# A WKV state stage with two gated layers on one core: the start and five steps ordered by hand, the weights' remainder and low bits on other engines

## The chip, the cores and the metric

The kernel runs on one core of one Trainium2 chip. The metric is the device time of one execution in microseconds (us). A profile of one execution is read beside it.

## What is computed

Three stages follow each other: a recurrence over 768 time steps for 4 batches and 8 heads of size 48, a layer with a hard gate, and a layer with a norm and a silu gate. Everything is in fp32.

```python
for t in range(S):                                   # S = 768, D = 48
    cur = einsum('bhd,bhe->bhde', u * k[t], v[t])
    y[t] = einsum('bhd,bhde->bhe', r[t], state + cur)
    state = w[t][..., None] * state + einsum('bhd,bhe->bhde', k[t], v[t])
x = y as (3072, 384)
h = x @ w_in                                         # 384 x 2048
x = (h * clip(h + 3, 0, 6) / 6) @ w_out              # 2048 x 384
xn = x / sqrt(mean(x * x) + 1e-6) * rms_g
g = xn @ w_gate                                      # 384 x 1536
out = (silu(g) * (xn @ w_val)) @ w_out2              # 1536 x 384
```

## The kernel before, in words

The 768 time steps are cut into six token blocks c of 128 steps; with four batches b that is 24 state blocks (class `Job`, block c, batch b), and 512 tokens for each c. A state block runs: `scans` (two running products of w on VectorE), `muls` (r and k scaled by them, VectorE), `fill` (ScalarE writes the diagonal into the matrix a, eight heads), `pe_a` (products of r and k on TensorE, in the PSUM tile aps), `choose` (VectorE copies the valid triangle of aps into a), `pe_y` (TensorE), `copy_y` and `split`. The state itself is added to by `pe_kt`, `copy_kt`, `pe_u` and `add_u`, and scaled by `decay` on GpSimd. For c = 0 there is no earlier state: `pe_y0` and `split_y0` take the place of `pe_y`, `copy_y` and `split`, and the bonus comes from `pairs` and `pe_bonus`.

Each fp32 matmul operand is used as a pair, a rounded high part and the remainder. A product is then three matmuls (`PASS`: high x high, high x remainder, remainder x high), nine for three slices of 128. Activations are split by `emit_split` (high copy on ScalarE, subtraction on GpSimd). The weights are stored as 64-bit floats: the input arrays are bits, and class `Weight` rebuilds the fp32 value of a 128x768 slice from two 32-bit words. `load` (SP queue) fetches `raw` (two buffers). `scale` is a ScalarE product of the high word into `mag` (one buffer). `bits` has three VectorE operations: the low word shifted right by 29 (line 143), the sign bit (line 144), and the shifted `mag` joined to it (line 146), in `x` (two buffers). `parts` writes the high copy (ScalarE, line 151) and the remainder (GpSimd, line 152) into `wpair` or `bpair`. There are 16 slices for the first layer (`wa`), 18 for the second (`wb`).

The first layer goes in steps n, one for each block c and slice f (128 of the 2048 columns): `ff1` (nine matmuls into hps, line 342; relu on ScalarE, line 348; product on VectorE, line 349; split) and, two steps later, `ff2` (nine matmuls into the three accumulators o, line 361). `LAGS` = (5, 8, 0, 0, 0, 0): in the first token block slices 0 to 4 are run first for tokens 0 to 255 (steps 0 to 4), then for tokens 256 to 511 (steps 5 to 9), as half steps; steps 10 to 20 take all 512 tokens. Step 21 is the first of the second token block.

The order on each engine is written out by hand. `pin` chains all instructions of an engine in the order in which the program emits them, and each engine works through its queue in that order. Ahead of the loop three `run` lines order state blocks 0 and 1 and weights 0 and 1. In the loop the lists `before[n]`, `between[n]` and `behind[n]` say what is emitted ahead of step n's matmuls, behind its split, and behind the older step's `ff2`. `plan(j, n)` puts a state block of c > 0 into them: scans at n, products at n + 1, fill at n + 2, choose behind step n + 2, y at n + 3, split at n + 5. The blocks of c = 1 are planned at 11, 15, 19 and 23. `begun` gives the step in which a weight is rebuilt.

The six PSUM pools: ps_h two banks (hps, and yps of `pe_y0`), ps_o three (accumulators), ps_s one (small products), ps_a two (aps, yps).

In the sixth token block, and in the first gated one (lines 621 to 655), the slices of the second layer are rebuilt in the same way, among the steps.

Of the kernel before, what the change touches and what calls it, by code (L numbers as in the profile page):

```python
# [9 lines left out]
F32 = mybir.dt.float32  # L10
# [26 lines left out]
def kernel(  # L37
# [86 lines left out]
    class Weight:  # L124
# [11 lines left out]
        def scale(self):  # L136
            self.mag = st_p.tile([128, 2 * DM], F32, tag="mag", name="mag", bufs=1)
            nc.scalar.activation(out=self.mag, in_=self.words()[1].bitcast(F32), func=AF.Copy, scale=2.0 ** -112)  # L138

        def bits(self):  # L140
            low, high = self.words()
            x = st_p.tile([128, 2 * DM], U32, tag="x", name="x")
            nc.vector.tensor_scalar(x, low, 29, None, ALU.logical_shift_right)  # L143
            nc.vector.scalar_tensor_tensor(  # L144
                out=x, in0=high, scalar=0x80000000, in1=x, op0=ALU.bitwise_and, op1=ALU.bitwise_or)
            nc.vector.scalar_tensor_tensor(  # L146
                out=x, in0=self.mag.bitcast(U32), scalar=3, in1=x, op0=ALU.logical_shift_left, op1=ALU.bitwise_or)
            self.x = x.bitcast(F32).rearrange("p (a n) -> p a n", a=2)
# [9 lines left out]
    class Job:  # L158
# [19 lines left out]
        def scans(self):  # L178
            nc.vector.memset(dd[:, :, :, 0:1], 1.0)
            self.scan(0)  # L180
            self.s1, self.s2 = self.w[:, 0], self.w[:, 1]
            nc.vector.reciprocal(out=dd[:, :, :, 0:1], in_=self.s1[:, :, :, HF:HF + 1])
            self.scan(1)

# [61 lines left out]
        def pe_a(self):  # L246

            self.aps = ps_a.tile([128, 2, NP, CH], F32, tag="A", name="aps")
            for p in range(NP):
                for i in range(2):  # L250
                    nc.tensor.matmul(  # L251
                        self.aps[:, i, p, :], self.rk[64 * i:64 * i + D, p, 1:3, :].rearrange("p a j -> p (a j)"),
                        self.rk[64 * i:64 * i + D, p, 0:4:3, :], start=True, stop=True)

        def choose(self):
            for i in range(2):
                nc.vector.copy_predicated(
                    self.a[:, i], mask.unsqueeze(1).to_broadcast([128, NP, CH]), self.aps[:, i])
# [73 lines left out]
        def split_y0(self):  # L332
            xt = self.xt()
            nc.scalar.activation(out=xt[:, :, 0, :], in_=self.yps, func=AF.Copy)
# [10 lines left out]

    def emit_act(ps, n):
        a = rg_p.tile([128, n], F32, tag="a", name="a", bufs=2)
# [392 lines left out]
```

## Time and profile before

| | |
|---|---|
| time, median of 3 runs | 1035.52 us (1034.21 to 1036.18) |
| profiled execution | 1035.39 us, span 1033.6 us |
| TensorE busy | 972.1 us (94% of the span) |
| VectorE busy | 482.4 us |
| GpSimd busy | 441.8 us |
| ScalarE busy | 405.5 us |
| mean granted clock of TensorE | 0.969 |

The span runs from the first to the last instruction. In the profile PE is TensorE's matmuls, PEld its weight loads, DVE VectorE, ACT ScalarE, POOL GpSimd, SPq the DMA queue of SyncE. A busy share is an average over stages with different limits, so the stages are read one by one. A clock of 1.00 stands for 2.4 GHz, 0.50 for 1.2 GHz.

### The profile page before, as it was taken

Reading aid. Unit: us, or ns where it says so; the run is one execution under the profiler, and the core shown is the slowest. Engines: PE = TensorE matmul, PEld = TensorE weight load, DVE = VectorE, ACT = ScalarE, POOL = GpSimd, SP = SyncE. Lnnn points to the kernel's source line nnn. Section 1 sums busy time; section 2 is a strip of 40 time slices with the busy share of each in tenths; the row PEclk is TensorE's granted clock in tenths of the full one; section 3 lists DMA queues with packets and bytes.
Section 4 is the critical chain, followed back from the end, with each engine's and each line's share of the span. In section 5 each row is a group of like instructions: output and inputs, shape, how many; then the busy total and the mean of one; then the engine's idle time right before and its main releaser. Section 6 shows DMA issues by size and latency. Waiting matters only on the chain.

```text
span 1033.6 us, 14038 instructions
## 1 busy us (share of the span) xinstructions
PE 972.1 (94%) x5517; PEld 804.5 (78%) x5517; DVE 482.4 (47%) x597; ACT 405.5 (39%) x774; POOL 441.8 (43%) x361
## 2 busy tenths in 40 slices
PE   5588799899999999999998899999999999999998
PEld 4587588778888888877776677888888888888887
DVE  7858865564457556655378666412112112112111
ACT  3365365544544544454454535322222212222222
POOL 1346675455465665664375555411122112211121
PEclk9589889899999999999999989999999999999999
DMA  8236422434222422330333332010100100100000
GB/s 313 90 123 224 151 90 83 141 112 140 77 77 84 168 75 77 124 129 8 130 131 101 135 97 88 37 56 1 59 2 1 62 1 1 62 1 1 31 1 30
DMA packets 32417, 85.65 MB, mean 83 GB/s; under 512 B 5728, under 2 KB 12768, under 8 KB 32352
## 3 DMA queue, kind: packets, MB, share of 16 engines
q1 hardware_dynamic: 32352, 84.76, 23.7%
q8 instruction: 43, 0.70, 0.3%
q14 instruction: 22, 0.18, 0.0%
HBM read 71.37 MB, written 9.44 MB: 78 GB/s over the span
## 4 chain that ended last, share of the span: by engine, by line
PE 73%; DVE 10%; issue 6%; ACT 5%; POOL 2%; DMA 2%; SPq 1%; ACTq 0%; POOLq 0%; DVEq 0%
PE o L361 26%; PE hps L342 13%; PE gps L342 13%; PE vps L342 13%; DVE x L144 3%; PE aps L251 2%; PE yps L293 2%; DVE x L146 2%; DVE x L143 2%; ACT a L348 1%; POOL wpair L152 1%; DVE a L349 1%; PE yps L287 1%; ACT a L232 1%; DVE w L174 1%
## 5 line engine op out<-in xcount | busy, mean ns | idle before, releaser
L361 PE MATMUL o<-g,wpair 128*128 128x512 f32 (+1 forms) x1422 | 330.5, 377 | 1.8 <-DVE x L376 1.7
L361 PEld LDWEIGHTS o<-g,wpair 128*128 128x128 f32 x1422 | 252.6, 191 | 50.2 <-DVE x L376 2.1
L342 PE MATMUL hps<-xt,wpair 128*128 128x512 f32 (+1 forms) x981 | 221.5, 371 | 15.8 <-DVE a L349 8.7
L355 POOL TENSOR_TENSOR g<-a,g 128x512 fp32r<-128x512 f32 (+1 forms) x109 | 141.1, 1295 | 204.8 <-ACT g L354 194.4
L355 POOL TENSOR_TENSOR g<-s,g 128x512 fp32r<-128x512 f32 x72 | 95.8, 1330 | 299.1 <-ACT g L354 298.7
L342 PEld LDWEIGHTS hps<-xt,wpair 128*128 128x128 f32 x981 | 173.1, 193 | 49.5 <-DVE a L349 11.3
L636 DVE TENSOR_TENSOR s<-s,vps 128x512 f32<-128x512 f32 x72 | 49.5, 687 | 309.2 <-PE vps L342 289.8
L349 DVE SCALAR_TENSOR_TENSOR a<-a,hps 128x512 f32<-128x512 f32 (+1 forms) x109 | 67.5, 619 | 170.1 <-ACT a L348 170.0
L348 ACT ACTIVATE a<-hps,half 128x512 f32<-128x512 f32 (+1 forms) x109 | 68.6, 629 | 98.6 <-PE hps L342 93.9
L342 PE MATMUL gps<-xt,wpair 128*128 128x512 f32 x432 | 105.9, 389 | 0.0
L342 PE MATMUL vps<-xt,wpair 128*128 128x512 f32 x432 | 105.7, 389 | 0.0
L354 ACT ACTIVATE g<-a 128x512 fp32r<-128x512 f32 (+1 forms) x109 | 63.4, 581 | 107.6 <-DVE a L349 106.1
L354 ACT ACTIVATE g<-s 128x512 fp32r<-128x512 f32 x72 | 45.5, 632 | 146.1 <-DVE s L636 146.1
L633 ACT ACTIVATE s<-gps 128x512 f32<-128x512 f32 x72 | 42.9, 596 | 150.3 <-PE gps L342 150.3
L342 PEld LDWEIGHTS gps<-xt,wpair 128*128 128x128 f32 x432 | 81.0, 188 | 17.2 <-ACT s L633 0.5
L342 PEld LDWEIGHTS vps<-xt,wpair 128*128 128x128 f32 x432 | 81.1, 188 | 16.8
L152 POOL TENSOR_TENSOR wpair<-x,wpair 128x768 fp32r<-128x768 f32 x28 | 56.6, 2021 | 67.7 <-ACT wpair L151 67.7
L174 DVE TENSOR_TENSOR_SCAN w<-w,dd 128x520 f32<-128x520 f32 x48 | 80.0, 1666 | 4.5 <-DMA w<-in_dram 2.8
L361 PE MATMUL o<-g,bpair 128*128 128x512 f32 x216 | 55.2, 400 | 5.9 <-ACT x L378 3.8
L232 ACT ACTIVATE a<-iperm,cb 128x128 f32<-128x128 f32 x192 | 58.5, 387 | 0.1
L342 PE MATMUL gps<-xt,bpair 128*128 128x512 f32 x216 | 54.6, 398 | 0.2 <-ACT s L633 0.2
L138 ACT ACTIVATE mag<-raw 128x768 f32<-128x768 f32 x34 | 30.5, 897 | 59.1 <-issue 29.5
(75 smaller groups left out, 967.5 us busy)
## 6 DMA issues: line engine op xcount, KB each, us to landing
raw<-in_dram SPq DMA_DIRECT2D x34, 768.0 KB, 4.3
w<-in_dram SPq DMA_DIRECT2D x24, 520.0 KB, 3.8
rk<-in_dram SPq DMA_DIRECT2D x24, 512.0 KB, 4.5
rks<-in_dram SPq DMA_DIRECT2D x20, 384.0 KB, 4.7
v<-in_dram SPq DMA_DIRECT2D x24, 256.0 KB, 4.8
xn<-x SPq DMA_DIRECT2D x6, 768.0 KB, 4.3
xraw<-xn SPq DMA_DIRECT2D x6, 768.0 KB, 5.1
out_dram<-osb SPq DMA_DIRECT2D x15, 256.0 KB, 2.5
```

The source lines that it names most:

```text
L144: nc.vector.scalar_tensor_tensor(out=x, in0=high, scalar=0x80000000, in1=x, op0=ALU.bitwise_and, op1=ALU.bitwise_or)
L152: nc.gpsimd.tensor_tensor(out=self.dst[:, :, 1, :], in0=self.x, in1=self.dst[:, :, 0, :].bitcast(F32), op=ALU.subtract)
L174: nc.vector.tensor_tensor_scan(out=x, data0=x, data1=dd.rearrange("p a h j -> p (a h j)"), initial=0.0, op0=ALU.mult, op1=ALU.add)
L232: nc.scalar.activation(out=self.head(h), in_=iperm, func=AF.Copy, scale=self.cb[:, h, :])
L342: nc.tensor.matmul(ps, slot[:, l, k * 128:(k + 1) * 128], xt[:, k, r, :], start=(k == 0 and j == 0), stop=(k == KT - 1 and j == 2))
L348: nc.scalar.activation(out=a, in_=ps, func=AF.Relu, scale=1.0 / 6.0, bias=half)
L349: nc.vector.scalar_tensor_tensor(out=a, in0=a, scalar=1.0, in1=ps, op0=ALU.min, op1=ALU.mult)
L354: nc.scalar.activation(out=g[:, 0, :], in_=a, func=AF.Copy)
L355: nc.gpsimd.tensor_tensor(out=g[:, 1, :], in0=a, in1=g[:, 0, :].bitcast(F32), op=ALU.subtract)
L361: nc.tensor.matmul(acc[m][:, cols], slot[:, l, m * 128:(m + 1) * 128], g[:, r, :], start=(first and j == 0), stop=(last and j == 2), **kw)
L633: nc.scalar.activation(out=s, in_=gp, func=AF.Silu)
L636: nc.vector.tensor_tensor(out=s, in0=s, in1=vp, op=ALU.mult)
```

## The change

Six things are changed.

- The remainder of a weight (`rest`) is subtracted on VectorE; before it was on GpSimd (in `parts`).
- The low word's bits come from ScalarE: `scale` adds a Copy of byte 3 of each 64-bit element, times 1/32, minus 31/64, rounded to an integer into `x`. VectorE's `bits` has two operations, `sign` and `join`.
- The order ahead of the loop is written out anew, for all four state blocks of c = 0, five weights and the steps 0 to 4; the loop begins at step 5. A step is a class, `Step`, whose parts can be placed one by one.
- State block 1 has aps in two banks of the accumulators.
- `decay`, `pe_kt`, `copy_kt` of state blocks 0 to 3 stand at steps 5 to 8 (before: from step 1), `pe_u` and `add_u` one step later.
- The later weights are rebuilt at other steps (`begun`), with high copy and remainder two steps after the bits and ahead of the next weight's scaling; the state blocks of c = 1 are planned at 10, 14, 18 and 22.

```diff
         def scale(self):
             self.mag = st_p.tile([128, 2 * DM], F32, tag="mag", name="mag", bufs=1)
             nc.scalar.activation(out=self.mag, in_=self.words()[1].bitcast(F32), func=AF.Copy, scale=2.0 ** -112)
+            self.x = st_p.tile([128, 2 * DM], U32, tag="x", name="x")
+            top = self.raw.bitcast(mybir.dt.uint8).rearrange("p (n h) -> p n h", h=8)[:, :, 3]
+            nc.scalar.activation(out=self.x, in_=top, func=AF.Copy, scale=1.0 / 32, bias=-31.0 / 64)
+
+        def sign(self):
+            nc.vector.scalar_tensor_tensor(
+                out=self.x, in0=self.words()[1], scalar=0x80000000, in1=self.x,
+                op0=ALU.bitwise_and, op1=ALU.bitwise_or)
+
+        def join(self):
+            nc.vector.scalar_tensor_tensor(
+                out=self.x, in0=self.mag.bitcast(U32), scalar=3, in1=self.x,
+                op0=ALU.logical_shift_left, op1=ALU.bitwise_or)
+            self.x = self.x.bitcast(F32).rearrange("p (a n) -> p a n", a=2)
 
         def bits(self):
-            low, high = self.words()
-            x = st_p.tile([128, 2 * DM], U32, tag="x", name="x")
-            nc.vector.tensor_scalar(x, low, 29, None, ALU.logical_shift_right)
...
-        def parts(self):
+            self.sign()
+            self.join()
+
+        def high(self):
             nc.scalar.activation(out=self.dst[:, :, 0, :], in_=self.x, func=AF.Copy)
-            nc.gpsimd.tensor_tensor(
+
+        def rest(self):
+            nc.vector.tensor_tensor(
                 out=self.dst[:, :, 1, :], in0=self.x, in1=self.dst[:, :, 0, :].bitcast(F32), op=ALU.subtract)
...
         def pe_a(self):
-            self.aps = ps_a.tile([128, 2, NP, CH], F32, tag="A", name="aps")
+            if self.i == 1:
+                self.aps = [ps_o.tile([128, NP, CH], F32, tag=f"o{i}", name="aps") for i in range(2)]
+            else:
+                ps = ps_a.tile([128, 2, NP, CH], F32, tag="A", name="aps")
+                self.aps = [ps[:, i] for i in range(2)]
...
-    before[0] += [j2.pairs, j2.muls]
-    between[0] += [j2.pe_bonus, j2.fill, j2.pe_a]
-    before[1] += [j3.scans, j2.choose]
-    between[1] += [j2.pe_y0, j2.split_y0]
-    before[2] += [j3.pairs, j3.muls]
-    between[2] += [j3.pe_bonus, j3.fill, j3.pe_a]
-    behind[2] += [j3.choose]
-    between[3] += [j3.pe_y0, j3.split_y0]
-    for j, n in enumerate((1, 2, 3, 4)):
-        behind[n] += [jobs[j].decay]
-        between[n + 1] += [jobs[j].pe_kt, jobs[j].copy_kt]
-        between[n + 2] += [jobs[j].pe_u, jobs[j].add_u]
-    for j, n in zip(range(B, 2 * B), (11, 15, 19, 23)):
+    for j, n in enumerate((5, 6, 7, 8)):
+        behind[n] += [jobs[j].decay, jobs[j].pe_kt, jobs[j].copy_kt]
+        between[n + 1] += [jobs[j].pe_u, jobs[j].add_u]
+    for j, n in zip(range(B, 2 * B), (10, 14, 18, 22)):
         plan(j, n)
...
-    begun = {f: f - 2 for f in range(2, W1 + 1)} | {8: 7} | {f: f + 1 for f in range(9, F1)}
+    begun = {5: 5, 6: 7, 7: 9} | {f: f + 2 for f in range(8, F1)}
     for f, n in begun.items():
+        before[n + 2] += [wa[f].high, wa[f].rest]
         before[n] += [wa[f].scale]
         behind[n] += [wa[f].bits]
-        before[n + 1 if f < 5 else n + 2] += [wa[f].parts]
         if f + 2 < F1:
             behind[n] += [wa[f + 2].load]
-    behind[7] += [lambda: jobs[4].load("w", "rk", "rks", "v")]
-    behind[9] += [lambda: jobs[5].load("w", "rk", "v")]
+    behind[5] += [lambda: jobs[4].load("w", "rk", "rks", "v")]
+    behind[8] += [lambda: jobs[5].load("w", "rk", "v")]
...
-    run((j0.scans, j0.pairs, j0.pe_bonus, j0.muls, j0.fill, j0.pe_a, j1.scans, j1.pairs, j1.pe_bonus, j1.muls))
-    run((j0.choose, j1.fill, j1.pe_a, j0.pe_y0, wa[0].scale, wa[0].bits, j1.choose, j1.pe_y0))
-    run((j0.split_y0, wa[0].parts, wa[1].scale, wa[1].bits, j1.split_y0, j2.scans, wa[1].parts))
+    w0, w1, w2, w3, w4 = wa[:5]
+    line = [Step(*x) for x in steps]
+    s0, s1, s2, s3, s4 = line[:5]
+    run((j0.scans, j0.pairs, j0.pe_bonus, j0.muls, j0.fill, j0.pe_a))
+    run((j1.scans, j1.pairs, w0.scale, j1.pe_bonus, j1.fill, j1.muls, j1.pe_a))
+    run((w0.sign, j0.choose, w0.join, w2.load, w0.high, j0.pe_y0, j1.choose, j1.pe_y0))
+    run((w0.rest, j0.high_y0, j0.rest_y0, w1.scale, w1.sign, j1.high_y0, j1.rest_y0, s0.pe_h, s0.relu))
+    run((w1.join, w3.load, w1.high, j2.scan1, w1.rest, s1.pe_h, s0.act, s0.split, s1.relu, j2.scan2, j2.pairs))
+    run((j2.pe_bonus, w2.scale, j2.muls, j2.fill, j2.pe_a, w2.sign, w2.join, w4.load, s1.act, s1.split, w2.high))
+    run((j2.choose, j2.pe_y0, w2.rest, s2.pe_h, s2.relu, s0.pe_o, j3.scans, j2.high_y0, j2.rest_y0, j3.pairs))
+    run((j3.pe_bonus, w3.scale, j3.muls, j3.fill, j3.pe_a, s2.act, s2.split, w3.bits, wa[5].load, w3.high))
+    run((j3.choose, j3.pe_y0, w3.rest, s3.pe_h, s3.relu, s1.pe_o, w4.scale, w4.bits, wa[6].load, w4.high))
+    run((j3.high_y0, s3.act, s3.split, j3.rest_y0, w4.rest, s4.pe_h, s4.relu, s2.pe_o, s4.act, s4.split))
+    todo += [s3, s4]
     pin()
 
-    for n, (c, f, cols) in enumerate(steps):
-        if n == W1:
+    for n in range(LAGS[0], len(steps)):
+        c, f, cols = steps[n]
+        if n == 2 * LAGS[0]:
...
+            if f - 2 in begun2:
+                wb[begun2[f - 2]].high()
+                wb[begun2[f - 2]].rest()
             if f in begun2:
                 wb[begun2[f]].scale()
-            if f - 2 in begun2:
-                wb[begun2[f - 2]].parts()
```

In the gated block the second layer's `high` and `rest` likewise stand ahead of the next `scale`.

## Rows read from the trace of the kernel before

**Rows 1.** Busy time by stretch; columns: from:to, length, engines (count), clock, DMA.

```profile
core 0: us, PE busy (x) PEld busy (x) DVE busy (x) ACT busy (x) POOL busy (x), PEclk, DMA share, GB/s
...
23.00:68.20 45.20, 30.17 (x232) 26.49 (x233) 33.87 (x43) 19.93 (x45) 14.89 (x14) 0.70 0.27 89
...
82.30:151.00 68.70, 58.39 (x337) 46.99 (x336) 54.62 (x60) 33.57 (x61) 50.83 (x37) 0.88 0.46 164
...
250.00:600.00 350.00, 338.07 (x2010) 271.76 (x2009) 212.80 (x254) 170.08 (x325) 201.76 (x160) 0.99 0.31 105
```

**Rows 2.** Timeline (start, us, engine, line): first groups of steps 5, 10, 21.

```profile
68.17 1.24 PE L342 MATMUL hps<-xt,wpair 128*128 128x256 f32 x9
...
82.29 2.23 PE L342 MATMUL hps<-xt,wpair 128*128 128x512 f32 x9
...
150.94 1.23 PE L342 MATMUL hps<-xt,wpair 128*128 128x256 f32 x9
```

**Rows 3.** Chain that ended last, in order of time: start, us, what.

```profile
251.16 2.04 PE o L361 x9
```

**Rows 4.** Timeline, VectorE, line 349: products of steps 9, 13, 17, 20.

```profile
83.19 0.42 DVE L349 SCALAR_TENSOR_TENSOR a<-a,hps 128x256 f32<-128x256 f32 x1 [1.58 <-ACT a L348]
...
105.54 0.69 DVE L349 SCALAR_TENSOR_TENSOR a<-a,hps 128x512 f32<-128x512 f32 x1 [1.60 <-ACT a L348]
...
135.49 0.68 DVE L349 SCALAR_TENSOR_TENSOR a<-a,hps 128x512 f32<-128x512 f32 x1
...
149.88 0.69 DVE L349 SCALAR_TENSOR_TENSOR a<-a,hps 128x512 f32<-128x512 f32 x1 [1.72 <-ACT a L348]
```

**Rows 5.** Tile raw over the whole span: duration in ns, min/median/max.

```profile
L143 DVE TENSOR_SCALAR x<-raw x34: 546/556/1700, 15.0 to 640.4; 128x768 uint32<-128x768 uint32 x34
L144 DVE SCALAR_TENSOR_TENSOR x<-raw,x x34: 958/960/2487, 15.6 to 641.0; 128x768 uint32<-128x768 uint32 x34
L138 ACT ACTIVATE mag<-raw x34: 878/897/920, 17.2 to 636.2; 128x768 f32<-128x768 f32 x34
```

**Rows 6.** Timeline: one undisturbed instruction of each kind.

```profile
30.05 0.66 DVE L214 TENSOR_TENSOR rp<-rk 128x512 f32<-128x512 f32 x1
...
84.75 0.68 ACT L348 ACTIVATE a<-hps,half 128x512 f32<-128x512 f32 x1
...
130.12 1.82 POOL L152 TENSOR_TENSOR wpair<-x,wpair 128x768 fp32r<-128x768 f32 x1
...
137.22 0.83 ACT L151 ACTIVATE wpair<-x 128x768 fp32r<-128x768 f32 x1
...
151.15 2.44 ACT L232 ACTIVATE a<-iperm,cb 128x128 f32<-128x128 f32 x8
151.32 1.28 POOL L355 TENSOR_TENSOR g<-a,g 128x512 fp32r<-128x512 f32 x1 [0.62 <-ACT g L354]
...
153.20 0.66 PE L239 MATMUL ktp<-ident,rk 128*128 128x128 f32 x4
...
154.32 1.35 DVE L257 COPY_PREDICATED a<-mask,aps 128x512 f32<-128x512 uint32 x2
...
158.46 0.62 PE L266 MATMUL ups<-v,kt 128*64 128x48 f32 x16
...
159.25 1.01 POOL L201 TENSOR_TENSOR rks<-rks 128x384 f32<-128x384 f32 x1
...
161.46 1.24 DVE L174 TENSOR_TENSOR_SCAN w<-w,dd 128x520 f32<-128x520 f32 x1
```

**Rows 7.** Timeline: a bit operation of VectorE beside a GpSimd subtraction.

```profile
531.73 2.16 POOL L152 TENSOR_TENSOR bpair<-x,bpair 128x768 fp32r<-128x768 f32 x1
...
532.21 2.49 DVE L144 SCALAR_TENSOR_TENSOR x<-raw,x 128x768 uint32<-128x768 uint32 x1
```

**Rows 8.** Timeline, first gated block: change of blocks, then two weight scalings.

```profile
593.93 1.65 PE L361 MATMUL o<-g,bpair 128*128 128x512 f32 x3 [3.84 <-ACT x L378]
...
612.37 0.89 ACT L138 ACTIVATE mag<-raw 128x768 f32<-128x768 f32 x1 [4.15 <-issue]
...
620.54 0.89 ACT L138 ACTIVATE mag<-raw 128x768 f32<-128x768 f32 x1 [4.14 <-issue]
```

More of the change, by code (lines that the diff above doesn't have):

```diff
@@ L176, in scan, with scan1 @@
                 initial=0.0, op0=ALU.mult, op1=ALU.add)
-        def scans(self):
+        def scan1(self):
             nc.vector.memset(dd[:, :, :, 0:1], 1.0)
@@ L181, in scans, with scan2 @@
             self.s1, self.s2 = self.w[:, 0], self.w[:, 1]
+        def scan2(self):
             nc.vector.reciprocal(out=dd[:, :, :, 0:1], in_=self.s1[:, :, :, HF:HF + 1])
             self.scan(1)
+        def scans(self):
+            self.scan1()
+            self.scan2()
         def decay(self):
@@ L477, with __init__, pe_h, relu @@
     open_halves = False
-    def ff1(c, f, cols):
-        n = cols.stop - cols.start
-        ps = ps_h.tile([128, n], F32, tag="h", name="hps")
-        emit_h(wpair[f][:, 0], xts[c][:, :, :, cols], ps)
-        a = emit_act(ps, n)
-        g = emit_split(a, n)
-        todo.append(lambda: ff2(c, f, cols, g))
+    class Step:
+        def __init__(self, c, f, cols):
+            self.c, self.f, self.cols, self.n = c, f, cols, cols.stop - cols.start
+        def pe_h(self):
+            self.ps = ps_h.tile([128, self.n], F32, tag="h", name="hps")
+            emit_h(wpair[self.f][:, 0], xts[self.c][:, :, :, self.cols], self.ps)
+        def relu(self):
+            self.a = rg_p.tile([128, self.n], F32, tag="a", name="a", bufs=2)
+            nc.scalar.activation(out=self.a, in_=self.ps, func=AF.Relu, scale=1.0 / 6.0, bias=half)
+        def act(self):
+            nc.vector.scalar_tensor_tensor(
+                out=self.a, in0=self.a, scalar=1.0, in1=self.ps, op0=ALU.min, op1=ALU.mult)
+        def split(self):
+            self.g = emit_split(self.a, self.n)
+        def pe_o(self):
+            ff2(self.c, self.f, self.cols, self.g)
     def ff2(c, f, cols, g):
@@ L580 @@
                 part(f - 8)
+            if f - 2 in begun2:
+                wb[begun2[f - 2]].high()
+                wb[begun2[f - 2]].rest()
             if f in begun2:
                 wb[begun2[f]].scale()
-            if f - 2 in begun2:
-                wb[begun2[f - 2]].parts()
-        ff1(c, f, cols)
+        now = line[n]
+        run((now.pe_h, now.relu, now.act, now.split))
+        todo.append(now)
         run(between[n])
@@ L590 @@
             wb[begun2[f] + 2].load()
-        while len(todo) > 2:
-            todo.pop(0)()
+        if len(todo) > 2:
+            todo.pop(0).pe_o()
         run(behind[n])
@@ L615, in out2, with __init__, pe_o @@
             store(c, whole)
+    class Out:
+        def __init__(self, *args):
+            self.args = args
+        def pe_o(self):
+            out2(*self.args)
     outs = []
@@ L623 @@
             if c == 0:
+                if f < 2 and F1 + f - 2 in begun2:
+                    wb[begun2[F1 + f - 2]].high()
+                    wb[begun2[F1 + f - 2]].rest()
+                if 2 <= f < NB - NE + 2:
+                    wb[NE + f - 2].high()
+                    wb[NE + f - 2].rest()
                 if f < NB - NE:
                     wb[NE + f].scale()
-                if f < 2 and F1 + f - 2 in begun2:
-                    wb[begun2[F1 + f - 2]].parts()
-                if 2 <= f < NB - NE + 2:
-                    wb[NE + f - 2].parts()
             gp = ps_h.tile([128, TOK], F32, tag="h", name="gps")
```

29 lines of the change are left out of this document (9 added, 20 removed).

## The prediction

> **What bounds the kernel now.** I read the stages first [rows 1], then when the first matmul group of chosen steps starts [rows 2], then what each step waits for. From 250 us on TensorE is the bound: 338 of 350 us busy up to 600, at full clock, nine matmuls every 2.04 us [rows 1, 3]. A cheaper weight preparation gives back only the few holes there. The change can pay or cost where TensorE has holes: 30.2 us busy of 45.2 between 23 and 68.2 us, at a mean granted clock of 0.70, so in part at the lower level of 1.2 GHz, and 58.4 of 68.7 between 82.3 and 151, at 0.88. In both stretches VectorE is the busiest of the other engines (33.9 and 54.6 us) [rows 1].
>
> What sets the pace of steps 10 to 20 is read from the VectorE product of each step (line 349). It starts at 83.2 for step 9, at 105.5 for step 13, 135.5 for step 17 and 149.9 for step 20 [rows 4]: 66.7 us for eleven steps, 6.1 each, while a whole step's two matmul groups take 4.1 and the state work about 1 more. The pace is that of a loop between VectorE and ScalarE: there is one "mag" buffer, so ScalarE's scaling of the next weight waits for VectorE's last bit operation on this one (the join), and the next step's relu stands behind that scaling on ScalarE.
>
> **How I sum.** I listed each engine's instructions in program order. An instruction starts at the later of its engine's last end and its inputs' end, plus 0.05 to 0.1 us for a hand-over; durations are those of the rows [rows 3, 5, 6], and TensorE's are doubled after holes like those in which the old trace shows the lower level. For the old order this gives 72.1, 85.7 and 155.6 us for the starts of steps 5, 10 and 21, where the trace has 68.2, 82.3 and 150.9 [rows 2], and 1039.3 for the span of 1033.6: some 4 us too late by step 5, and little added from there. I use differences between my lists of the two orders.
>
> **Turns.** A bit operation that began at 532.21 lasted 2.49 instead of 0.96. It ended 0.81 after the GpSimd subtraction beside it (531.73 + 2.16 = 533.89) [rows 5, 7]. So the one that waits loses nearly all of the other's remaining time and gets 0.15 back; both lists let the two engines take turns like this wherever both read two SBUF inputs. The Trainium skill, "SBUF — State Buffer", section "Who interferes with whom", says that a VectorE instruction with two SBUF inputs and a GpSimd instruction that reads SBUF block each other for the whole instruction. This also speaks against a part of the change, since the moved subtraction has two SBUF inputs and now contends itself. Taken to the letter, without the 0.15, the difference of the two lists falls from +8.7 to +4.1 us; the trace shows the 0.15.
>
> **Part by part.**
>
> Weights, 34 of them. VectorE loses the low-word shift, 0.556, and gets the subtraction. A two-input product over 128x512 takes 0.66, so 0.99 for 768 columns by proportion; the two-input bit operation over 768 takes 0.96 [rows 5, 6]. I take 0.96, with 0.85 and 1.0 as bounds. GpSimd loses 1.82 [rows 6], and VectorE the turns against it. ScalarE gets a conversion of one byte per element. Nearest are the scaling with the same stride, 0.897, and the contiguous copy, 0.83; relu's 0.68 for 512 columns makes 1.02 by proportion [rows 5, 6]. I take 0.90, with 0.83 and 1.02 as bounds. Per weight that is VectorE +0.4 less up to 1.7 of turns, and ScalarE +0.9. But a wait is new: the low bits of weight f go into one of two x buffers, free only when VectorE's remainder of weight f-2 is done. That remainder stands on VectorE behind the state block's scans or products of the same step, and the step's relu stands behind the low bits on ScalarE.
>
> Start to step 5. The first group comes 2.4 us earlier (block 1's product has banks of its own, the remainder is on VectorE), the second 10.7 (the second scan of block 2 now stands behind it). Most of this is given back: at blocks 2 and 3 the engines wait for each other in a row of pairs, matmuls, cb copy, scaling, low bits, fill 2.44 [rows 6], choose, y's matmuls at the lower clock, next group, relu, and behind that on ScalarE the scaling of the fifth weight. Steps 2, 3 and 4 start at 40, 55 and 63 us in my list, step 5 at 67.9 against 72.1 in that of the old order: -4.2.
>
> Steps 5 to 9. The four put-off transposes and state products, 0.66 + 0.62 of TensorE each [rows 6], 5.1 together, now lie bare among half steps of 2 x 1.02; in the old loop they begin three steps earlier, among holes. Step 10 starts at 86.9 against 85.7, so this stage costs +5.3. SP's loads of the later weights and of block 4 move by a step or two with the weights and end no wait in the list.
>
> Steps 10 to 20, the term that decides. Take steps 14 to 17, one state block. Scan step: relu 0.68, product 0.69, sign 0.96, GpSimd's turn 1.28, join 0.96, two scans 2.48 with some 0.3 around them, two turns of 1.01 for the bonus products, remainder 0.96, low bits 0.90: 11.2, less 0.15 for each of five turns, 10.4. Next step: two products 1.32 and a reduction of about 0.5 (384 columns, by proportion) in place of scans and bonus: 8.3. Fill step, along ScalarE: product 0.69, g copy 0.6, fill 2.44, high copy 0.83, scaling 0.90, low bits 0.90, relu 0.68: 7.0. Choose step: relu 0.68, product 0.69, choose 1.35 (GpSimd's turn lies beside it), sign, join and remainder 2.88, low bits 0.90: 6.5 [rows 4 to 6]. Together 32.2, in the list with hand-overs 33.3, where the old trace has 30.0 (105.5 to 135.5). By the same sums steps 10 to 13 come to 29.0 (no remainder is due in step 10, so its scans cost 6.6) against 22.3, and steps 18 to 20 to 17.9 against 14.4. That is 80.2 against 66.7; from the start of step 10 to that of step 21 it is +14.4 between the lists.
>
> Second token block. Its state blocks are planned one step earlier than now, so its waits for xt get shorter: -2.1. From there to the last block TensorE covers everything: 0.
>
> Last block and first gated block, where the second stage's weights are made. Last block: +1.4, from ScalarE's extra conversions. Gated: the old loop takes 8.2 from scaling to scaling (612.37 to 620.54), longer than three groups (6.1), and a hole of 3.84 lies at the change of blocks [rows 3, 8]. New loop: scaling 0.90, low bits 0.90, silu as relu 0.68, product 0.69, sign 0.96, turn 1.28, join 0.96: 6.4, so TensorE is nearly at its own pace again: -6.1.
>
> Sum: -4.2 + 5.3 + 14.4 - 2.1 + 1.4 - 6.1 = +8.7. On the profiled execution's 1035.39 (span 1033.6 and 1.8 around it; the median is 1035.52, so there is nothing to correct) this makes 1044.1. The bounds through the list: remainder at 0.85, -2.5; low bits at 0.83, -2, at 1.02, +4.6; turns to the letter, -4.6. With what both lists share as error, 1037.5 to 1053.
>
> **The rivals.** First, faster: the loop doesn't close, because VectorE is far enough ahead that the remainder of f-2 is done before ScalarE asks for its buffer. Then VectorE's sum paces steps 14 to 17: 4 x (0.69 + 2.88) + 2.8 + 1.3 + 0.5 + 1.35 + 0.3 = 20.5, and turns 4 x 1.28 + 2.0 - 0.9 = 6.2, so 26.7, some 6.5 less than I have, 3 less in steps 10 to 13 and 2 in the last three: 1032.5, and down to 1026 where half of the turns fall into VectorE's own waits. For it: GpSimd, busy 50.8 of 68.7 us there [rows 1], is relieved of 1.82 a weight. Against it: scans and products stand ahead of the remainder in program order. It decides in step 14, by whether ScalarE waits before its low bits.
>
> Second, much slower: a byte at a stride of eight costs ScalarE 1.15 or more, and TensorE drops to the lower clock in more of the longer holes. The list gives +9.6 more with 1.15: 1053 to 1058.
>
> Third, gains and losses cancel: the start gains 3 us more than I count, where my list is at its worst, and steps 10 to 20 lose half: 1033.5 to 1037.5.
>
> The skill's turn rule to the letter (1039.5) lies inside the forecast.
>
> **How the numbers follow.** Forecast (1037.5 to 1053) 0.57, much slower 0.13, no change within 0.2% (2 us, about what a measurement of this kernel can tell) 0.12, faster 0.18. Slower is 0.57 + 0.13 = 0.70. The range leaves about a tenth out on each side: 1029 to 1056.
>
> **What would show it.** Right: step 5 starts at 62 to 66 us, step 10 near 83; the products of steps 13 and 17 lie over 31 us apart; ScalarE's idle time before the low bits is put down to VectorE's remainder; step 21 starts after 160; the gated block's scalings come every 6 to 7 us. Wrong: step 21 before 152, or low bits that never wait; then the first rival holds. If the start alone is off by more than 5 us, it is TensorE's clock that I mis-sized.

## The result and the profile after

The changed kernel takes 1042.0 us (median; 1041.2 to 1043.3) against 1035.5 of the kernel before (1034.2 to 1038.0): ratio 1.0062, 95% interval 1.0046 to 1.0078. It is slower by 6.5 us, inside the forecast of 1037.5 to 1053. The profiled span is 1040.2 against 1033.6, +6.6.

The same stretches as in [rows 1], a little shifted since the steps moved. Columns: from:to, length, busy time and count of each engine, granted clock, share of DMA, GB/s.

```profile
core 0: us, PE busy (x) PEld busy (x) DVE busy (x) ACT busy (x) POOL busy (x), PEclk, DMA share, GB/s
23.00:62.00 39.00, 23.63 (x171) 19.10 (x171) 25.89 (x37) 16.88 (x38) 3.56 (x4) 0.72 0.25 84
62.00:82.00 20.00, 17.93 (x144) 16.91 (x145) 7.87 (x11) 10.68 (x21) 5.27 (x8) 0.77 0.50 179
82.00:160.00 78.00, 60.90 (x356) 47.54 (x355) 60.97 (x66) 43.54 (x74) 31.60 (x26) 0.85 0.41 138
250.00:600.00 350.00, 344.27 (x2087) 277.14 (x2083) 211.80 (x255) 177.65 (x334) 177.23 (x150) 1.00 0.30 102
```

From 250 to 600 us TensorE is still the bound (344 of 350 us). From 82 to 160 us, which ends before step 20 does, GpSimd fell to 31.6 us of 78 (in [rows 1] 50.8 of 68.7), ScalarE rose to 43.5 (33.6 of 68.7), and TensorE is busy for 60.9 of 78 us, at 0.85 of full clock.

Where single steps start, timeline of the changed kernel, in the order of [rows 2]: the first matmuls of steps 5, 10 and 21.

```profile
66.05 1.96 PE L365 MATMUL hps<-xt,wpair 128*128 128x256 f32 x9
...
85.85 2.23 PE L365 MATMUL hps<-xt,wpair 128*128 128x512 f32 x9
...
166.84 1.23 PE L365 MATMUL hps<-xt,wpair 128*128 128x256 f32 x9
```

Step 5 starts 2.1 us earlier than before, step 10 3.6 later, step 21 15.9 later. The product of VectorE (now line 500) in steps 9, 13, 17 and 20, beside [rows 4]:

```profile
86.51 0.42 DVE L500 SCALAR_TENSOR_TENSOR a<-a,hps 128x256 f32<-128x256 f32 x1 [1.01 <-ACT a L497]
...
114.82 0.69 DVE L500 SCALAR_TENSOR_TENSOR a<-a,hps 128x512 f32<-128x512 f32 x1 [1.55 <-ACT a L497]
...
147.14 0.69 DVE L500 SCALAR_TENSOR_TENSOR a<-a,hps 128x512 f32<-128x512 f32 x1 [1.54 <-ACT a L497]
...
164.09 0.69 DVE L500 SCALAR_TENSOR_TENSOR a<-a,hps 128x512 f32<-128x512 f32 x1 [4.10 <-ACT a L497]
```

Steps 10 to 13 take 28.3 us (22.3 before, 29.0 forecast), steps 14 to 17 32.3 (30.0; 33.3), steps 18 to 20 17.0 (14.4; 17.9). Rows of step 14, from the timeline of all engines but DMA and weight loads:

```profile
117.76 1.73 POOL L218 TENSOR_TENSOR rks<-rks 128x384 f32<-128x384 f32 x1
...
118.67 1.92 DVE L185 TENSOR_TENSOR_SCAN w<-w,dd 128x520 f32<-128x520 f32 x1
...
119.56 1.81 POOL L219 TENSOR_TENSOR rks<-rks,ub 128x384 f32<-128x384 f32 x1
119.59 0.61 PE L365 MATMUL hps<-xt,wpair 128*128 128x512 f32 x2
...
120.86 1.61 DVE L185 TENSOR_TENSOR_SCAN w<-w,dd 128x520 f32<-128x520 f32 x1
...
122.39 0.93 DVE L163 TENSOR_TENSOR wpair<-x,wpair 128x768 fp32r<-128x768 f32 x1
...
123.35 0.90 ACT L142 ACTIVATE x<-raw 128x768 uint32<-128x768 uint8 x1 [3.75 <-DVE wpair L163]
...
123.37 3.35 PE L365 MATMUL hps<-xt,wpair 128*128 128x512 f32 x7 [3.16 <-DVE wpair L163]
...
124.15 0.67 ACT L497 ACTIVATE a<-hps,half 128x512 f32<-128x512 f32 x1
```

Two things wait here for the same remainder (122.39), which stands behind two scans on VectorE. One is the wait I forecast: ScalarE's low bits (line 142), idle for 3.75 us before them, with the relu of step 14 (124.15) behind them. The other I did not name: TensorE itself. Of the nine matmuls of step 15 it has done the first two, which need only the weight's high part (119.59), and stands 3.16 us for the remainder. The waits of the changed kernel from 82 to 170 us, by engine and line (us in total, times, longest), show both:

```profile
PE hps L365 <- DVE wpair L163: 12.2, 5, 4.4
...
ACT x L142 <- DVE wpair L163: 6.8, 5, 3.8
```

In the kernel before, no matmul waits for a weight in that stretch. Which of the two costs the time is what the experiments have to tell.

The prices were right. Whole span (ns, min/median/max): the low bits take 0.89 us where I had taken 0.90; the remainder (tile wpair, VectorE) 0.956 in the median, where I had 0.96.

```profile
L142 ACT ACTIVATE x<-raw x34: 870/891/907, 14.2 to 639.8; 128x768 uint32<-128x768 uint8 x34
...
L163 DVE TENSOR_TENSOR wpair<-x,wpair x28: 925/956/2054, 19.3 to 652.4; 128x768 fp32r<-128x768 f32 x28
```

### The profile page after: what moved, and what is told of

It reads as the page before. It is cut to its first block, busy times and chain, and to the rows that moved or that the text cites. A ratio compares the mean times of both kernels' runs of the same rounds, so it can differ in the third digit from the quotient of the medians.

```text
span 1040.2 us, 14044 instructions
## 1 busy us (share of the span) xinstructions
PE 974.0 (94%) x5517; PEld 802.7 (77%) x5517; DVE 480.8 (46%) x597; ACT 432.3 (42%) x808; POOL 365.7 (35%) x327
## 4 chain that ended last, share of the span: by engine, by line
PE 73%; DVE 5%; issue 4%; ACT 4%; DMA 1%; SPq 1%; POOL 1%; ACTq 0%; POOLq 0%; DVEq 0%
PE o L378 27%; PE gps L365 14%; PE vps L365 14%; PE hps L365 12%; PE yps L314 2%; PE aps L272 2%; PE yps L308 1%; DVE x L145 1%; ACT a L497 1%; DVE x L150 1%; DVE a L500 1%; DMA x<-y 1%; DVE w L185 1%; PE ktp L256 1%; SPq L326 1%
## 5 line engine op out<-in xcount | busy, mean ns | idle before, releaser
L365 PE MATMUL hps<-xt,wpair 128*128 128x512 f32 (+1 forms) x981 | 227.8, 377 | 28.3 <-DVE wpair L163 14.4
L372 POOL TENSOR_TENSOR g<-a,g 128x512 fp32r<-128x512 f32 (+1 forms) x109 | 133.0, 1220 | 310.7 <-ACT g L371 294.8
L372 POOL TENSOR_TENSOR g<-s,g 128x512 fp32r<-128x512 f32 x72 | 92.7, 1288 | 344.0 <-ACT g L371 344.0
L185 DVE TENSOR_TENSOR_SCAN w<-w,dd 128x520 f32<-128x520 f32 x48 | 76.8, 1599 | 4.5 <-DMA w<-in_dram 2.8
L150 DVE SCALAR_TENSOR_TENSOR x<-mag,x 128x768 uint32<-128x768 uint32 x34 | 57.5, 1690 | 1.1
L365 PE MATMUL vps<-xt,bpair 128*128 128x512 f32 x216 | 52.9, 389 | 0.0
```

The lines of the kernel that those rows point to most:

```text
L150: nc.vector.scalar_tensor_tensor(out=self.x, in0=self.mag.bitcast(U32), scalar=3, in1=self.x, op0=ALU.logical_shift_left, op1=ALU.bitwise_or)
L185: nc.vector.tensor_tensor_scan(out=x, data0=x, data1=dd.rearrange("p a h j -> p (a h j)"), initial=0.0, op0=ALU.mult, op1=ALU.add)
L365: nc.tensor.matmul(ps, slot[:, l, k * 128:(k + 1) * 128], xt[:, k, r, :], start=(k == 0 and j == 0), stop=(k == KT - 1 and j == 2))
L372: nc.gpsimd.tensor_tensor(out=g[:, 1, :], in0=a, in1=g[:, 0, :].bitcast(F32), op=ALU.subtract)
```

## The experiments

Theory A is that of the prediction: the weight split (low bits on ScalarE, remainder on VectorE) closes a loop through the x buffers and ScalarE's queue, which costs the time in steps 10 to 20. Rival O: the order of the steps costs it (weights begun at step f+2 instead of f+1, additions put off, state blocks a step earlier). Rival S: VectorE's sum is the pace. Medians are set against the kernel before, run beside them on the same chip. What a run gains on the changed kernel is, unless two times are given, the difference of these two differences.

**Low bits back on VectorE.**

```diff
-            nc.scalar.activation(out=self.x, in_=top, func=AF.Copy, scale=1.0 / 32, bias=-31.0 / 64)
...
         def sign(self):
+            self.x = st_p.tile([128, 2 * DM], U32, tag="x", name="x")
+            nc.vector.tensor_scalar(self.x, self.words()[0], 29, None, ALU.logical_shift_right)
```

> The changed kernel, but the low word's three bits are made by VectorE's shift again (0.556 us a weight), not by ScalarE (0.89). All else stays, the remainder on VectorE too. Theory (the x buffer closes a loop through ScalarE's queue: low bits of weight f wait for VectorE's remainder of f-2, and the relu behind them waits too): the wait leaves ScalarE's queue, and ScalarE loses 0.89 a weight. By the list, against the changed kernel: start of step 10 -3.9, of step 21 -9.0, gated block another -5, end -15.2, so 1042.0 - 15.2 = 1026.8; products of steps 13 and 17 29.9 apart (changed kernel 33.3 in the list, 32.3 on the chip). Rival 1 (the hand-written order costs the time, the weight split does not): within 2 us of 1042. Rival 2 (VectorE's sum is the pace): 11 to 16 weights times 0.56 more on VectorE, 1048 to 1051.

Measured: 1030.9, ratio 0.9951 (0.9936 to 0.9965), 11 us faster than the changed kernel. VectorE has more work (73.3 us busy from 82 to 170 against 63.4) and the kernel is faster: S falls. The low bits are a cause. But TensorE still waits as long for weights in that stretch:

```profile
PE hps L364 <- DVE wpair L162: 12.8, 4, 5.3
```

**Remainder back on GpSimd, low bits left on ScalarE.**

```diff
         def rest(self):
-            nc.vector.tensor_tensor(
+            nc.gpsimd.tensor_tensor(
```

> The changed kernel, but the weight remainder is GpSimd's again (1.82 us), and the low bits stay on ScalarE. Theory (loop through x): the remainder now also stands behind GpSimd's g remainder and bonus products and takes twice as long, so x comes free later: by the list step 21 +8.2, end +14.0, so 1056; products of steps 13 and 17 37.1 apart. Rival 1 (order alone): within 2 us of 1042. Rival 2 (VectorE's sum is the pace): 0.96 less on VectorE for each of 34 weights, of which 11 lie in steps 10 to 20: 10 us faster there less new turns of up to 1.82 each, 1032 to 1042.

Measured: 1055.6, ratio 1.0192 (1.0160 to 1.0224), as A expected. S falls again: VectorE is relieved and the kernel is slower. The run does not tell the two waits on the remainder apart: from 82 to 170 us TensorE waits 19.7 us for GpSimd's remainder, and ScalarE's low bits 12.1.

**Both back: the new order with the old way of making weights** (the two edits above together).

> The changed kernel's order of all steps, with the weights made as before: shift on VectorE, remainder on GpSimd. Theory (the weight split closes the loop, the order alone costs little): by the list step 21 -4.9, end -8.4, so 1033.6, within 2 us of the kernel before; products of steps 13 and 17 31.7 apart. Rival 1 (order alone costs it): 1042 +- 2. Rival 2 (VectorE's sum): VectorE gains 0.96 and loses 0.556 a weight, 1036 to 1040.

Measured: 1039.2, ratio 1.0034 (1.0022 to 1.0047). This lies between A (1033.6) and O (1042), and the starts of the steps (table below) speak for O: from step 9 to step 21 this order loses 14.8 us with the old weights, more than the changed kernel itself loses there (11.4). The list had step 21 4.9 us earlier than in the changed kernel; it came 1.0 earlier. There is no low-bit conversion and no x loop through ScalarE in this run. TensorE waits for weights all the same, now for GpSimd's remainder, 82 to 170 us:

```profile
PE hps L364 <- POOL wpair L162: 16.9, 5, 5.0
```

**High copy and remainder ahead of the state work of their step.**

```diff
-        before[n + 2] += [wa[f].high, wa[f].rest]
+        before[n + 2][0:0] = [wa[f].high, wa[f].rest]
```

> The changed kernel, with the high copy and the remainder of the weight issued ahead of the state block's scans or products in the same step (from step 7 on), nothing else. It takes the 2.8 us of scans and 1.8 of products out from between x's last reader and the low bits that wait for x. Theory (loop through x, remainder behind the scans): by the list step 21 -7.2, part of it given back in the next block, end -5.2, so 1036.8; products of steps 13 and 17 30.4 apart (33.3 in the list for the changed kernel). Rival 1 (order of the first steps, put-off additions): within 1 us of 1042. Rival 2 (VectorE's sum is the pace, whatever its order): within 1.5 us of 1042.

Measured: 1039.5, ratio 1.0032 (1.0021 to 1.0043): 2.7 us of the 5.2 expected. Among the waits of this run from 82 to 170, ScalarE's low bits no longer wait for the remainder, and TensorE's wait for it is 4.6 us in place of 12.2 (but 5.9 for the high copy, where the changed kernel has 3.2). The step that A rests on exists, but it is worth half.

**Three x buffers for the first stage.**

```diff
-            self.x = st_p.tile([128, 2 * DM], U32, tag="x", name="x")
+            self.x = st_p.tile([128, 2 * DM], U32, tag="x", name="x", bufs=3 if self in wa else 2)
```

> The changed kernel with three x buffers in place of two for the first stage's weights, nothing else. Theory (low bits of weight f wait in ScalarE's queue for VectorE's remainder of f-2, through the x buffer): with a third one they wait for the remainder of f-3, long done. By the list the start of step 21 comes 5.6 us earlier, the products of steps 13 and 17 lie 29.7 apart (33.3 in the list for the changed kernel, 32.3 on the chip) and the end is 5.6 earlier: 1042.0 - 5.6 = 1036.4; ScalarE's waits before the low bits for VectorE's remainder vanish. Rival 1 (what costs is the order: weights made one step later, closer to their use, and the state additions put off): within 1.5 us of 1042. Rival 2 (VectorE's sum): within 1.5 us of 1042.

Measured: 1039.6, ratio 1.0031 (1.0017 to 1.0045), 2.9 us of the 5.6 expected. The wait of the low bits is gone altogether; what stays, 82 to 170 us, is TensorE's:

```profile
PE hps L365 <- DVE wpair L163: 11.7, 4, 4.4
```

So the x buffers alone are worth some 3 us of the whole, not the +14.4 that I had put to their loop.

**Three x and two mag buffers for the first stage.**

```diff
-    nm_p = pool(ctx, "nm", side="left")
...
-            self.mag = st_p.tile([128, 2 * DM], F32, tag="mag", name="mag", bufs=1)
+            self.mag = st_p.tile([128, 2 * DM], F32, tag="mag", name="mag", bufs=2 if self in wa else 1)
...
-            self.x = st_p.tile([128, 2 * DM], U32, tag="x", name="x")
+            self.x = st_p.tile([128, 2 * DM], U32, tag="x", name="x", bufs=3 if self in wa else 2)
...
+            nm_p = pool(ctx, "nm", side="right", reuse_waits="tile")
```

> As the kernel with three x buffers, and with two mag buffers besides, both for the first stage's weights alone (the norm's buffers move to other addresses to make room). Theory (two loops through single buffers; the one through mag takes over when the one through x is open): the list gives 0 for a second mag buffer alone, and -11.2 for both, with the start of step 21 at -11.2: 1030.8; products of steps 13 and 17 28.2 apart. Rival 1 (the order alone, or weights that are made too near to their use): 1036 to 1042. Rival 2 (VectorE's sum): 1040 to 1042.

Measured: 1035.4, ratio 0.9996 (0.9982 to 1.0010): no difference from the kernel before, 7.1 us better than the changed kernel where the list has 11.2. A second mag buffer, which the list prices at nothing by itself, gives 4 more once x is open. It was not run by itself in the new order, and the move of the norm's buffers was not run by itself either.

**Old weights in the new order, begun one step earlier.**

```diff
-    begun = {5: 5, 6: 7, 7: 9} | {f: f + 2 for f in range(8, F1)}
+    begun = {5: 5, 6: 6, 7: 8} | {f: f + 1 for f in range(8, F1)}
```

> The changed order with the weights made as before (shift on VectorE, remainder on GpSimd), as in the run that gave 1039.2, and now with the weights from 6 on begun one step earlier (step f+1 in place of f+2, as the old kernel does from weight 9 on). Theory (part of the loss is the order: a weight is ready one step before its use instead of two, so that each late part stops TensorE): by the list -5.9, so 1033.3; step 21 6 us earlier than in that run. Rival (the loss of that run lies in the put-off additions and the state blocks one step earlier): 1038 to 1040.

Measured: 1034.6, ratio 0.9992 (0.9979 to 1.0005), 4.8 us better than the run of the old weights, each against its own kernel before. This is O's part, and it shows where it should: from step 9 to 36 the loss falls from 11.2 to 3.2 us, and of TensorE's 16.9 us of waits for GpSimd's remainder 0.7 are left, 82 to 170 us:

```profile
PE hps L364 <- POOL wpair L162: 0.7, 2, 0.4
```

**The kernel before with two mag buffers** (four constant tables moved to another pool).

```diff
-            self.mag = st_p.tile([128, 2 * DM], F32, tag="mag", name="mag", bufs=1)
+            self.mag = st_p.tile([128, 2 * DM], F32, tag="mag", name="mag", bufs=2)
...
```

> The kernel before with two mag buffers in place of one in both stages (four constant tables move to another pool to make room), nothing else. Theory (in the old order the loop between VectorE's join and ScalarE's next scaling through the one mag buffer sets the pace in steps 10 to 20 and in the gated block): by the list step 21 2.9 earlier and the gated block 12 shorter, end -15.3, so 1020.2; as the list makes the old gated block 3.7 us too long (88.8 to the second block of groups, 85.1 on the chip), 1020 to 1025. Rival 1 (VectorE's sum is the pace in steps 10 to 20, TensorE in the gated block): 1034 to 1036. Rival 2 (earlier scalings only make ScalarE's relu wait longer): 1036 to 1039.

Measured: 1024.1, ratio 0.9891 (0.9864 to 0.9918). The loop through mag that I read in the old profile is real, but it alone does not set the pace of steps 10 to 20, as the prediction has it: opening it gives 2.8 us from step 9 to step 21, which are some 70 us long. It gives 4.2 us up to step 21, 5.3 in the last token block and 1.7 in the first gated block; I had looked for most of it in the gated block. There the scalings of this run come 6.6 us apart in the mean (572.52 to 618.53, seven intervals), where the old kernel has 7.7 (582.11 to 636.21, seven) with 8.2 between those of [rows 8]; three of them:

```profile
597.58 0.89 ACT L138 ACTIVATE mag<-raw 128x768 f32<-128x768 f32 x1
603.70 0.89 ACT L138 ACTIVATE mag<-raw 128x768 f32<-128x768 f32 x1
610.22 0.89 ACT L138 ACTIVATE mag<-raw 128x768 f32<-128x768 f32 x1 [0.30 <-DMA raw<-in_dram]
```

**The whole split in the old order** (low bits on ScalarE and remainder on VectorE in the kernel before).

```diff
+            nc.scalar.activation(out=self.x, in_=top, func=AF.Copy, scale=1.0 / 32, bias=-31.0 / 64)
...
-            nc.vector.tensor_scalar(x, low, 29, None, ALU.logical_shift_right)
...
-            nc.gpsimd.tensor_tensor(
+            nc.vector.tensor_tensor(
                 out=self.dst[:, :, 1, :], in0=self.x, in1=self.dst[:, :, 0, :].bitcast(F32), op=ALU.subtract)
...
```

> The kernel before with the weight split of the change alone: low bits on ScalarE, remainder on VectorE, in the old order of steps (in the last and the gated block the high copy and remainder of an earlier weight go ahead of the next scaling, as in the change, since the two x buffers demand it). Theory (the split closes a loop through ScalarE's queue in steps 10 to 20, in any order of steps): by the list the start of step 21 comes 6.5 us later than in the kernel before, the gated block gives 5 back, end +1.7 on 1035.5: 1037.2. Rival 1 (the whole loss is the order): 1028 to 1034, the split alone is a gain. Rival 2 (the losses of order and split add: order alone was 3.4 over the kernel before, both are 6.3 over it): 1038.4; this lies near the first, and the start of step 21 tells more than the time.

Measured: 1031.6, ratio 0.9960 (0.9945 to 0.9975): the split by itself is a gain of 4.8 us, as O's rival says and A does not. Yet its low bits wait for the remainder as much as in the changed kernel (6.8 us, 5 times), 82 to 170 us:

```profile
ACT x L141 <- DVE wpair L154: 6.6, 4, 3.8
```

The same wait stands in a kernel that is 4.8 us faster and in one that is 6.5 slower than the kernel before. Here no matmul waits for a weight. The wait still has a price: from step 9 to 36 this run loses 4.2 us, where the remainder alone, next, wins 0.9.

**The remainder alone in the old order.**

```diff
-            nc.gpsimd.tensor_tensor(
+            nc.vector.tensor_tensor(
                 out=self.dst[:, :, 1, :], in0=self.x, in1=self.dst[:, :, 0, :].bitcast(F32), op=ALU.subtract)
```

> The kernel before with the weight remainder on VectorE, and nothing else: the shift stays on VectorE, so ScalarE's queue holds no wait for x. Theory (the remainder on VectorE is a gain, since GpSimd's 1.82 and its turns go; only the low bits on ScalarE turn it into a loss): by the list end -5.4, so 1030.1, start of step 21 1.2 earlier, the gated block 5 shorter. Rival 1 (VectorE's sum is the pace in steps 10 to 20): 0.96 less turns of up to 0.9 a weight, 1035 to 1042. Rival 2 (the first rival of the prediction, VectorE far enough ahead): 1028 to 1032 too, but with most of the gain by step 21.

Measured: 1029.2, ratio 0.9929 (0.9910 to 0.9948). So in the old order the remainder is worth -7.2 us and the low bits +2.4, with the moved high copy and remainder of the run above counted in. In the new order the same two are worth -8.3 (1030.9 against 1039.2) and +11. The sign is the theory's, the place is not: the gated block is 1.2 us shorter in the profile where the list had 5, and 2.5 of the profiled run's 4.6 us are there by step 21, so the second rival is not excluded.

**Additions of the first block early** (three of the four batches).

```diff
-    for j, n in enumerate((5, 6, 7, 8)):
+    for j, n in ((3, 5),):
...
+    run((j0.decay, j0.pe_kt, j0.copy_kt))
...
+    run((j0.pe_u, j0.add_u, j1.decay, j1.pe_kt, j1.copy_kt))
...
+    run((j1.pe_u, j1.add_u, j2.decay, j2.pe_kt, j2.copy_kt))
...
+    run((j2.pe_u, j2.add_u))
```

> The changed kernel with the first block's transposes and state products for three of the four batches issued in the written-out steps 2 to 4, not in steps 5 to 8 (the fourth stays at step 5). Theory (they lie bare among half steps, 1.28 of TensorE each, but in steps 2 to 4 they stand in the row of pairs, so nothing is gained): by the list step 5 starts 4.7 later, step 10 1.5 earlier, step 21 1.0 later, end +1.0: 1043. Rival (the put-off additions are the +5.7 us that steps 5 to 9 lost, and nothing hides them): 3.8 us of TensorE come out of steps 5 to 9 and fall into holes, 1037 to 1039.

Measured: 1042.1, ratio 1.0056 (1.0041 to 1.0071), the time of the changed kernel. Step 5 is 5.4 us later, and step 9 is where it was: the three additions cost the start what steps 5 to 9 save. Putting them off neither cost nor saved anything.

**All three opened: shift on VectorE, weights a step earlier, two mag buffers** (the edits above together).

> The changed kernel without its low bits on ScalarE (shift on VectorE again, remainder still on VectorE), with weights from 6 on begun one step earlier, and with two mag buffers in both stages. Theory (three loops: x through ScalarE's queue, a weight ready one step before its use, mag through the scaling): each opened, by the list step 21 starts 16 us earlier than in the changed kernel, the gated block is 10 shorter, end -27, so 1015; by the differences measured so far one by one (-11.1 for the low bits, -4.5 for the earlier weights, up to -7 for mag in the gated block) 1019 to 1022. Rival (one cause, seen three times: the sum of the three is no more than the largest alone): 1027 to 1031.

Measured: 1015.9, ratio 0.9807 (0.9790 to 0.9823), faster than both kernels; 27 us less than the changed kernel, which is the list's own figure. The rival, one cause seen three times, falls. The second mag buffer in it is no part of the change, and gave the kernel before 11.9 us too. The changed kernel with its weights a step earlier, and nothing else, was not run.

**Where each run stands.** From the timelines: start of the relu of a step (of silu in the gated blocks), less that in the kernel before, us. The last column holds to the end. One profiled execution each, so a difference of a us or two in a column says little.

| run | step 5 | step 9 | step 21 | step 36 | gated block 0 | gated block 1 |
|---|---|---|---|---|---|---|
| changed kernel | -1.5 | +3.3 | +14.7 | +10.1 | +9.9 | +6.6 |
| old weights, new order | -3.6 | -1.1 | +13.7 | +10.1 | +8.9 | +5.4 |
| the same, weights earlier | -4.9 | -0.3 | +5.0 | +2.9 | +1.7 | -1.3 |
| low bits on VectorE | -6.0 | -3.5 | +5.6 | +1.4 | -1.4 | -5.1 |
| remainder on GpSimd | -1.9 | +1.6 | +20.9 | +16.4 | +16.5 | +17.4 |
| remainder ahead of the state work | -0.2 | +3.5 | +11.2 | +8.9 | +8.9 | +5.4 |
| three x | -0.0 | +3.6 | +12.8 | +8.7 | +8.6 | +5.4 |
| three x, two mag | -1.2 | +3.7 | +8.9 | +5.1 | +4.8 | +0.9 |
| additions early | +3.9 | +3.5 | +14.9 | +10.6 | +10.2 | +6.9 |
| old order, whole split | -1.3 | -1.3 | +3.4 | +2.9 | +2.6 | -1.4 |
| old order, remainder | -1.5 | -1.7 | -2.5 | -2.6 | -3.4 | -4.6 |
| old order, two mag | -1.4 | -1.4 | -4.2 | -4.3 | -9.6 | -11.3 |
| all three opened | -5.1 | -2.7 | -2.2 | -6.0 | -15.2 | -20.3 |

The products of steps 13 and 17 lie 30.0 us apart with the low bits on VectorE (expected 29.9), 36.4 with the remainder on GpSimd (37.1), 31.0 with it ahead of the state work (30.4), 30.8 with three x (29.7), 28.9 with two mag besides (28.2), and 33.3 with the old weights, where the list had 31.7. Only with the old weights, where the order stands alone, is the list short by more than 1.1.

## Why the prediction was right, and where it was not

Time and sign were right: +6.5 measured against +8.7. That the sum came so near is in part luck: the terms of steps 5 to 9 and of steps 10 to 20 have more causes than I gave them, and the errors of the terms offset each other. Term by term, from first groups as in [rows 2] up to step 21, from the relu at step 36, and from the first group of each gated block (573.15 and 658.29 before, 582.48 and 664.88 after): start to step 5 -2.1 (forecast -4.2), steps 5 to 9 +5.7 (+5.3), steps 10 to 20 +12.3 (+14.4), second block -5.8 (-2.1), to the last block 0 (0), last block -0.8 (+1.4), gated block -2.7 (-6.1). The sum is +6.6, that of the spans.

The marks: step 5 at 66.05 lies at the edge of 62 to 66, just outside; step 10 at 85.85 is 3 us past "near 83"; the products of steps 13 and 17 lie 32.3 apart; ScalarE's idle time before the low bits is put down to the remainder; step 21 is at 166.84; the scalings of the gated block come 6.8 us apart in the mean (591.26 to 638.69, seven intervals).

**Steps 10 to 20, the cause.** This is the step that failed. Its size was near, but I gave the whole of it to the split and the x buffers. The runs give the x buffers 3 us (three x, remainder first), and the new order by itself, with the old weights, loses as much between steps 9 and 21 as I had summed (14.8). From there the remainder on VectorE gives 5.7 back (9.1, low bits on VectorE) and the low bits take 2.3 (11.4, the changed kernel). The list held the order too, since I only ever compared it whole; I never took one part out of it before I named the cause. What the order does, from weight 7 on: a weight begins at step f+2 and its remainder is issued at f+4, one step ahead of its first use at f+5, where the old order leaves two. On VectorE it stands behind two scans, and TensorE stops in the middle of a group. Beginning the weights a step earlier takes 8.0 of 11.2 us out of steps 9 to 36; this was run with the old weights alone. The 3.2 left are the state blocks a step earlier, or the rest of the order; that was not separated.

**The mark that misled.** "ScalarE waits before its low bits" came true and decided against the first rival, as I had said it should. It stood as well, 6.6 us long, in the run of the split in the old order, which is a gain. A wait that the forecast names shows that the loop is there, not what it costs.

**Low bits.** Their price was right at 0.89, their place was not. In the new order they cost 11 us, of which 6.8 lie ahead of step 9 (the changed kernel against low bits on VectorE, +3.3 and -3.5), in the written-out steps where ScalarE's fill, copies and scalings stand in a row; I had counted that row, but named its cost only in the start, and gave all of +5.3 in steps 5 to 9 to the put-off additions. Without the low bits the relu of step 9 loses 2.5 on that of step 5, with them 4.8; the early-additions run shows that the place of the additions changes nothing by step 9. That row of operations as the reason for the 6.8 is my reading; no run took it apart.

**Steps 5 to 9.** That +5.7 lies so near +5.3 is luck. I counted all four pairs of transpose and state product as new, 5.1 us; but the old steps 5 to 9 hold one of the transposes and two of the products, so only 3 x 0.66 + 2 x 0.62 = 3.2 us are. About 2 us more are TensorE's lower level, 1.2 GHz, which that term does not name. This is an estimate from three rows: the group at 66.05 takes 1.96 where [rows 2] have 1.24, the group at 78.08 takes 2.27 where that at 82.83 takes 1.31, and the state product at 80.28 takes 1.10 where that at 84.08 takes 0.67. The granted clock is 1.00 in the old steps 5 to 9 (68.17 to 82.29) and 0.87 in the new ones (66.05 to 85.85). It is at 0.50 from 62 to 66 us, where TensorE had stood 3.98 and then 1.80 us for the parts of a weight, and from 78 to 80, where it had stood 1.60 us for a copy of ScalarE:

```profile
77.58 0.85 PE L256 MATMUL ktp<-ident,rk 128*128 128x128 f32 x4 [1.60 <-ACT st L294]
...
78.08 2.27 PE L365 MATMUL hps<-xt,wpair 128*128 128x256 f32 x9
...
82.83 1.31 PE L365 MATMUL hps<-xt,wpair 128*128 128x256 f32 x9
```

With the low bits on VectorE the same steps (62.29 to 79.83) are granted 1.00 and take 3.4 us more than before in place of 5.7.

**Second block.** The reason fits (work done a step ahead comes back), its size is over twice as large: from step 21 to 36 the runs of the new order give back 2.1 to 4.6 us, the two splits in the old order 0.1 and 0.5. I read this as state work already done, which step 21 shows as loss; the state blocks were not moved by themselves.

**Last block.** Here the sign of the term was wrong, -0.8 against +1.4. By the table, from step 36 to the first gated block, the changed kernel gains 0.2 us and the one with the low bits on VectorE 2.8: the low bits cost 2.6 there, more than I had. What offsets them I had not counted: the new order with the old weights gains 1.2, and the remainder on VectorE 1.6 more.

**Gated block.** The size of the term was off, not its direction. The list makes the old block 88.8 us long, the chip 85.1; less its 6.1 the new one would be 82.7, and the chip has 82.4. [rows 8] show a loop of 8.2 us on ScalarE, and I took its length for TensorE's; but the old kernel's gate groups start 6.3 apart in the mean from 608.11 to 658.29 (eight steps), little above their own 6.1. In these eight steps the change gives 0.7 (615.43 to 664.88); the other 2.0 lie ahead of them, at the change of blocks.

The rivals: the faster one fell at steps 13 to 17 (32.3, not 26.7); the much slower one at the low bits' 0.89, under its 1.15; the third needed half of steps 10 to 20 to vanish, and 12.3 of 14.4 stayed.

## What to carry to other kernels

Split a forecast loss by taking one part of the change out of the sum at a time before giving it a cause: here two parts that were each worth little by themselves (+3.4 the order, -4.8 the split) made +6.5 together. Look first at how many steps lie between the end of a buffer's making and its first use: with one left, TensorE waited 16.9 us for GpSimd's remainder here, with two 0.7, and the kernel was 4.8 us faster. A wait in the profile is no price until a run without it has been timed: a third x buffer removed 6.8 us of waits and gained about 3. A term that comes out near its forecast is no proof of its cause either: that of steps 5 to 9 did, with the clock in it unnamed.

## What the runs showed of the hardware

The step 14 rows show the turns of VectorE and GpSimd again, and both ways. The first scan, 1.24 undisturbed [rows 6], ended at 120.59, 1.10 after GpSimd's product (117.76 + 1.73 = 119.49), so it got 0.14 back. The GpSimd product at 119.56, 1.01 undisturbed (the first product in [rows 6], this one at 220.84 in the changed kernel), ended at 121.37, 0.78 after the first scan, and got 0.23 back. The Trainium skill, "SBUF — State Buffer", section "Who interferes with whom", lets a VectorE instruction with two SBUF inputs contend with a GpSimd instruction that reads SBUF, and calls the port pair that they share an exclusive lock; these rows agree but for that 0.14 to 0.23.

A higher granted clock came with little gain in one run. From 82 to 170 us the run with the remainder ahead of the state work was granted 0.96:

```profile
82.00:170.00 88.00, 68.74 (x471) 54.05 (x471) 67.75 (x75) 49.47 (x90) 39.83 (x34) 0.96 0.38 131
```

and the changed kernel 0.86:

```profile
82.00:170.00 88.00, 70.90 (x455) 55.90 (x453) 63.36 (x70) 49.44 (x89) 35.58 (x32) 0.86 0.37 123
```

The first is 2.7 us faster in the end. I read this as a stretch whose pace TensorE does not set; the edit moved the waits too, no run changed the clock alone, and so this is not shown.
